# Making the low halves of the output projection's weights on VectorE, not with adding DMAs

## The chip, the cores and the metric

The kernel runs on one core of one Trainium2 chip. A core has TensorE (PE: matmuls, with a separate weight load, PEld), VectorE (DVE), ScalarE (ACT), GpSimd (POOL) and SyncE (SP); they run side by side, each through its own list of instructions in order, and wait for each other by semaphores. DMAs are issued from the queues of SP, ACT and POOL; those that add to what stands at their target are issued by POOL. Matmuls read SBUF and write PSUM, which has eight banks here of 128 x 512 numbers. The metric is device microseconds of one execution, and less is better.

## The reference

All arrays are 32-bit floats. x has 2048 tokens of 512 numbers. Two branches are computed from it and mixed token by token with a gate:

```python
g = sigmoid((x * gate_w).sum(-1, keepdims=True))
a = A(x, wqkv, wo)      # attention: 32 heads of 16; each token sees itself and the 7 tokens
                        # 2, 4, ..., 14 places back; softmax; then (heads side by side) @ wo
b = (gelu(x @ w_gate) * (x @ w_up)) @ w_down      # inner width 1792
out = g * a + (1 - g) * b
```

wo, with which this change deals, is 512 x 512: the output projection of the attention.

## The kernel before, in words

**Two-part products.** [...] Each product is three matmuls: high x high, high x low, low x high. So every weight and every intermediate result that goes into a matmul is first split, by one of two ways:
- `split` (lines 86 to 94): ScalarE copies the number into the high tile (L90, or L135 where the copy is made by `held`), then VectorE subtracts high from number into the low tile (L91).
- `split_by_dma` (lines 232 to 236): ScalarE writes the negated number's high part into the low tile (L234), a DMA issued by POOL adds the number to it (L235), and ScalarE copies the high part (`held`, L135). VectorE has no part in it.

**Stages.** Tokens are worked on in two halves (`par` 0 and 1). For each: keys and queries, values, and the feed-forward (`ffn`, 14 blocks of its inner width), in which the gate and up products (`product`, L781, in a scheme of Strassen's kind with seven products per block) and the down products (`down`, L830) alternate. Four PSUM banks named p serve these products in turn and four named acc collect. A p bank is free again when ScalarE has copied it out: by L786, L792, L882 or L898 after the gate and up products, by L845 after a group of down products. L824 is the other way: ScalarE fills a p bank from SBUF so that a further group of down products can add to it.

**Attention** is VectorE's: `scores`, `exps`, `shares` and `mix` handle a unit of 128 columns (8 heads) at a time, four units per half. `attention` is a generator, pulled piece by piece (`pull`) by the feed-forward, and fills VectorE beside the matmuls. `mix` multiplies the shares with v (L585), sums (L589, L591, L593), and after each half unit transposes (L598) and writes the result to DRAM (SP's queue, L600, four DMAs). v has one buffer, which SP loads for the next unit (L523, L524) once the reading of the last one is over.

**Output projection.** `fetch_o` brings wo into one of the two buffers named raw. `load_o`, a generator that is pulled during the last feed-forward block, splits its four parts of 128 rows (units u = 0 to 3), two into a g1 buffer and two into S buffers. `channels` loads a unit's attention result from DRAM (L1040, SP's queue, into the next raw buffers) and splits it (L90, L91). `out_first` projects the first half of the tokens, `finish` the second half: there the matmuls of `by_unit` (L1062) add to the banks that hold the feed-forward's result, and the very last ones are those of unit 3.

The buffers named raw are two. The one with wo in it becomes free when the last split of wo has read it, and takes the results of the attention after that.

**What sets the order.** The kernel is written with a scheduling layer: the order in which instructions stand in the code gives priorities, a model of times inside that layer orders each engine's list, and it adds the waits. `paced` ties an instruction to the last matmul written so far, `keep_in_program_order` and `behind` pin single ones. So one instruction more or less moves others on all engines from that place on. Everything before the split of wo stands in the same order in both versions.

Of the kernel before, what the change touches and what calls it, by code (L numbers as in the profile page):

```python
# [48 lines left out]
def tile_gated_mix(ctx: ExitStack, tc: tile.TileContext, xt, wqkv, wff, wo, out):  # L49
    nc = tc.nc  # L50
# [10 lines left out]
    def tl(tag, dt=F32):  # L61
        return pool.tile([P, COLS.get(tag, 512)], dt, name=tag, bufs=BUFS[tag])

    def pair(tag):
        t = tl(tag, F32R)
        return t[:, :512], t[:, 512:1024]
# [19 lines left out]
    def split(eng, hi, lo, raw, copy=None, pinned=False):  # L86
        if copy:
            copy(hi, raw)
        else:
            nc.scalar.activation(hi, raw, AF.Copy)  # L90
        ins = eng.tensor_tensor(lo, raw, hi.bitcast(F32), op=OP.subtract)  # L91
        if pinned or PIN[0]:
            tc.keep_in_program_order(ins)
        return ins
# [39 lines left out]
    def held(o, i):  # L134
        ins = paced(nc.scalar.activation(o, i, AF.Copy))  # L135
        LAST_HI[:] = [ins]
        return ins
# [94 lines left out]
    def split_by_dma(hi, lo, raw):  # L232

        paced(nc.scalar.activation(lo, raw, AF.Copy, scale=-1.0))  # L234
        nc.gpsimd.dma_start(lo.bitcast(F32), raw, accum_op=OP.add)  # L235
        held(hi, raw)
# [371 lines left out]
    def paced(ins):  # L608

        if PIN[0] and ins.ins.engine == mybir.EngineType.DVE:  # L610
            tc.keep_in_program_order(ins)
        if not PACING[0]:
            return ins
        tc.add_manual_dep(ins.ins, LAST[-1].ins.name, mybir.DependencyInfo(mybir.DependencyClass.Sync,
                          mybir.DependencyReason.SCHED_ONLY), reason="pace")
        return ins
# [167 lines left out]
    def copy(ps):  # L784
        s = tl("s")
        nc.scalar.activation(s, ps, AF.Copy)  # L786
        return s
# [160 lines left out]
    def ffn(par):  # L948
        todo = iter(())
        for f in range(FC):  # L950
# [23 lines left out]
            if par:  # L974
                if f + 2 < FC:
                    at(0, fetch_sums, f + 2)
                else:
                    at(0, fetch_o) if f + 2 == FC else None
                if f + 1 == FC:
                    todo = chain(load_o(), channels_of(0, 0))  # L980
                    for i in range(1, 9):
                        at(i, next, todo, None)
            else:
                if f + 2 < FC:
                    at(1, fetch, f + 2)
                    at(8, combine, f + 2)
                else:
                    at(0, fetch_x, 1, f + 2 - FC)
                if f + 1 < FC:
                    do.setdefault(0, []).insert(0, lambda: keep(f + 1))  # L990
                at(0, keep_parts, f)
                if f + 2 == FC:
                    at(8, early)
                if f + 1 == FC:
                    todo = before()
                    for i in range(2, 9):
                        at(i, next, todo, None)
# [26 lines left out]
    def load_o():  # L1024
        t = tl("g1", F32R)
        cols = [t[:, i * 512:(i + 1) * 512] for i in range(4)]
        for u in range(NU):
            raw = WO[u]
            WO[u] = hi, lo = pair("S") if u > 1 else cols[2 * u:2 * u + 2]
            split_by_dma(hi, lo, raw)  # L1030
            yield

    OR = []
# [89 lines left out]
    for kc in range(KC):  # L1123
# [4 lines left out]
        raw = QR[name, i] = spare[i] if kc > 1 else tl("rt")  # L1128
# [218 lines left out]
```

## Time and profile before

| | |
|---|---|
| median of 3 runs | 596.75 us (595.22 to 597.41) |
| profiled execution | 597.42 us |
| its span, first to last instruction | 595.4 us |
| TensorE busy | 587.3 us, 99% |
| VectorE busy | 532.3 us, 89% |
| ScalarE busy | 427.5 us, 72% |
| mean granted clock of TensorE | 0.996 |
| DMA, mean | 240 GB/s |

How to read the lines that follow in the prediction: in a timeline, a line has the start and the duration in microseconds, the engine (PEq, SPq and so on are the queue's own issuing), the line of the code, the operation, the tile it writes and those it reads (without buffer numbers), and the count where several equal ones follow each other. In brackets stands the idle time of the engine just before it and what ended it. Starts of neighbours on one engine lie closer than the durations say, since an engine starts the next instruction before the last one is through. A chain of waits goes back from the last instruction to what released it, step by step. A line of the view by windows gives busy time and count per engine in that stretch, and the clock that TensorE was granted, as a share of full speed.

### The profile page before, as it was taken

What the parts mean: (1) busy time and instruction counts of PE and PEld (TensorE: products, weight loads), DVE (VectorE), ACT (ScalarE), POOL (GpSimd) and SP (SyncE); (2) the same over time, 40 slices, a digit from 0 to 9 for tenths busy, and PEclk for the clock granted to TensorE, in tenths of its full rate; (3) what the DMA queues carried; (4) which work ended last, traced back from release to release, by engine and by line L of the source; (5) the groups of instructions that cost most, each with busy time, mean ns of one, the idle gap of its engine ahead of it and who ended that gap; (6) DMA issues with size and microseconds to landing.
All of it is one profiled execution on the core that took longest, in us unless ns stands there. A gap on an engine that the chain in (4) does not pass through costs nothing.

```text
span 595.4 us, 8273 instructions
## 1 busy us (share of the span) xinstructions
PE 587.3 (99%) x2743; PEld 489.9 (82%) x2743; DVE 532.3 (89%) x623; ACT 427.5 (72%) x756; POOL 130.2 (22%) x157
## 2 busy tenths in 40 slices
PE   8999999999999999999999999999999999989997
PEld 6889888888888888888799888888888888868885
DVE  6889998999899995998997999998999899897871
ACT  6777667778887779877777665778767867795432
POOL 0140751112111212113120860112111113131300
PEclk9999999999999999999999999999999999998999
DMA  8689999988987979899999999869798988568934
GB/s 306 217 248 280 299 310 226 304 197 233 282 218 232 266 213 255 245 253 347 273 267 355 225 270 272 260 167 275 176 273 242 217 251 214 159 132 213 187 71 159
DMA packets 88424, 142.76 MB, mean 240 GB/s; under 512 B 8639, under 2 KB 49983, under 8 KB 88382
## 3 DMA queue, kind: packets, MB, share of 16 engines
q1 hardware_dynamic: 65454, 103.21, 52.3%
q0 software_dynamic: 22640, 38.64, 35.3%
q8 instruction: 21, 0.34, 0.2%
q10 hardware_dynamic: 288, 0.39, 0.2%
q14 instruction: 21, 0.17, 0.1%
HBM read 69.83 MB, written 46.49 MB: 195 GB/s over the span
## 4 chain that ended last, share of the span: by engine, by line
PE 95%; ACT 3%; DMA 1%; SPq 0%; issue 0%; ACTq 0%
PE p L781 43%; PE p L830 13%; PE acc L830 12%; PE acc L478 10%; PE p L1062 6%; PE p L364 4%; PE acc L364 3%; PE p L478 2%; PE acc L1062 2%; DMA raw<-xt 1%; ACT A L90 1%; ACT L898 0%; SPq L1132 0%; ACT g L234 0%; ACT hh L807 0%
## 5 line engine op out<-in xcount | busy, mean ns | idle before, releaser
L781 PE MATMUL p<-S,g 128*128 128x512 f32 x672 | 167.0, 389 | 0.0
L781 PEld LDWEIGHTS p<-S,g 128*128 128x128 f32 x672 | 125.8, 188 | 25.8
L781 PE MATMUL p<-A,g 128*128 128x512 f32 x504 | 125.8, 389 | 0.0
L781 PEld LDWEIGHTS p<-A,g 128*128 128x128 f32 x504 | 94.4, 188 | 19.8 <-ACT rt L845 0.3
L585 DVE TENSOR_TENSOR prod<-v,lg 128x2048 f32<-128x2048 f32 x32 | 72.7, 2273 | 2.3 <-DMA v<-vs 2.1
L542 DVE TENSOR_REDUCE lg<-prod 128x128 f32<-128x2048 f32 x32 | 73.0, 2281 | 0.2
L539 DVE TENSOR_TENSOR prod<-kq 128x2048 f32<-128x2048 f32 x32 | 72.9, 2277 | 0.2
L830 PE MATMUL p<-d,hh 128*128 128x512 f32 x224 | 68.5, 389 | 0.0
L830 PE MATMUL acc<-d,hh 128*128 128x512 f32 x224 | 59.2, 389 | 0.0
L740 POOL DMA_DIRECT2D g<-raw x26 | 23.6, 907 | 160.2 <-ACT g L737 103.6
L792 ACT ACTIVATE c<-p 128x512 f32<-128x512 f32 x56 | 33.4, 597 | 34.0 <-PE p L781 33.9
L830 PEld LDWEIGHTS acc<-d,hh 128*128 128x128 f32 x224 | 42.0, 188 | 8.7
L830 PEld LDWEIGHTS p<-d,hh 128*128 128x128 f32 x224 | 42.0, 188 | 8.8
L830 PE MATMUL p<-d,hl 128*128 128x512 f32 x112 | 42.1, 389 | 0.0
L793 DVE TENSOR_TENSOR c<-c,s 128x512 f32<-128x512 f32 x56 | 37.8, 681 | 4.6 <-ACT c L792 4.2
L797 DVE TENSOR_TENSOR c<-c 128x512 f32<-128x512 f32 x56 | 38.1, 683 | 2.1 <-ACT c L898 2.0
L589 DVE TENSOR_TENSOR prod<-prod 128x1024 f32<-128x1024 f32 x32 | 38.9, 1217 | 0.1
L845 ACT ACTIVATE rt<-p 128x512 f32<-128x512 f32 x48 | 27.7, 595 | 15.0 <-PE p L830 14.8
L786 ACT ACTIVATE s<-p 128x512 f32<-128x512 f32 x56 | 33.2, 595 | 5.5 <-PE p L781 5.1
L478 PE MATMUL acc<-d,S 128*128 128x512 f32 x144 | 35.6, 390 | 0.1
L772 POOL DMA_DIRECT2D d<-r x23 | 19.8, 859 | 68.9 <-ACT d L771 41.7
L830 PE MATMUL acc<-d,hl 128*128 128x512 f32 x112 | 34.6, 389 | 0.0
(223 smaller groups left out, 1068.3 us busy)
## 6 DMA issues: line engine op xcount, KB each, us to landing
g<-raw POOLq DMA_DIRECT2D x26, 512.0 KB, 6.7
ws<-g SPq DMA_DIRECT2D x14, 768.0 KB, 6.2
g<-ws SPq DMA_DIRECT2D x14, 768.0 KB, 6.6
r<-wff SPq DMA_DIRECT2D x28, 256.0 KB, 4.2
raw<-wff SPq DMA_DIRECT2D x14, 512.0 KB, 4.6
d<-r POOLq DMA_DIRECT2D x23, 256.0 KB, 6.6
ws<-raw SPq DMA_DIRECT2D x14, 384.0 KB, 5.7
raw<-ws SPq DMA_DIRECT2D x14, 384.0 KB, 3.8
```

The source lines that it names most:

```text
L364: LAST[:] = [nc.tensor.matmul(ps[:, :n], x[:, ts], VO[b][w][:, kc * WQ:kc * WQ + n], start=first, stop=(kc == 1 and i == 2), skip_group_ch ...
L478: LAST[:] = [nc.tensor.matmul(ps, x[:, ts], w, start=(start and kc == i == 0), stop=(kc == 1 and i == 2), skip_group_check=True)]
L539: paced(nc.vector.tensor_tensor(prod, spans(k, jj), q[:, jj:jj + 2, None, :].to_broadcast([P, 2, W, UC]), op=OP.mult))
L542: nc.vector.tensor_reduce(two_of(lg, jj), prod.rearrange("p j w (h d) -> p (j w) h d", d=DH), axis=AX.X, op=OP.add)
L585: paced(nc.vector.tensor_tensor(prod.rearrange("p j w (h d) -> p (j w) h d", d=DH), spans(v, jj).rearrange("p j w (h d) -> p j w h d", d=D ...
L589: nc.vector.tensor_tensor(prod[:, :, :4], prod[:, :, :4], prod[:, :, 4:], op=OP.add)
L781: LAST[:] = [nc.tensor.matmul(ps, w_, a_, start=(start and kc == 0 and n == 0), stop=(kc == 1 and n == 2), skip_group_check=True)]
L792: nc.scalar.activation(c, ps, AF.Copy)
L793: nc.vector.tensor_tensor(c, c, s, op=OP.add)
L797: nc.vector.tensor_tensor(ge, ge, up, op=OP.mult)
L830: LAST[:] = [nc.tensor.matmul(pp, a[:, ts], w, start=(i == 0 and n == 0 and gr == 0), stop=(i == 1 and n == 2), skip_group_check=True)]
L1062: LAST[:] = [nc.tensor.matmul(pa, a, b, start=(first and n == 0), stop=(last and n == 2), skip_group_check=True)]
```

## The change

`load_o` calls `split` with VectorE's subtraction in place of `split_by_dma`, with the same copy (`held`) for the high part. For each of the four parts of wo the negating copy L234 on ScalarE and the adding DMA L235 on POOL's queue are gone, and one subtraction L91 on VectorE is there.

```diff
         for u in range(NU):
             raw = WO[u]
             WO[u] = hi, lo = pair("S") if u > 1 else cols[2 * u:2 * u + 2]
-            split_by_dma(hi, lo, raw)
+            split(nc.vector, hi, lo, raw, held)
             yield
```

```python
    def split(eng, hi, lo, raw, copy=None, pinned=False):
        if copy:
            copy(hi, raw)
        else:
            nc.scalar.activation(hi, raw, AF.Copy)
        ins = eng.tensor_tensor(lo, raw, hi.bitcast(F32), op=OP.subtract)
...
    def split_by_dma(hi, lo, raw):

        paced(nc.scalar.activation(lo, raw, AF.Copy, scale=-1.0))
        nc.gpsimd.dma_start(lo.bitcast(F32), raw, accum_op=OP.add)
        held(hi, raw)
```

The lists of instructions are the same up to the first of these, and differ from there to the end. Three places:

TensorE, where the last gate and up products end and the output projection begins (both versions in one, - for before and + for now; g_5106 is the last block's weight, g_5191 the first two parts of wo, A the attention's result, d and hh, hl the operands of the down products):

```order
 L781 MATMUL p<-S,g_5106 128x512 x6
+L830 MATMUL p<-d,hh 128x512 x2
+L830 MATMUL p<-d,hl 128x512
+L830 MATMUL p<-d,hh 128x512 x2
+L830 MATMUL p<-d,hl 128x512
 L1062 MATMUL p<-g_5191,A 128x512 x6
 L1062 MATMUL p<-S,A 128x512 x5
```

A group of six down products, which stood behind the first two groups of the projection, now comes ahead of them.

ScalarE at the same place, before (S_5253 is the last part of wo, p_5205 and p_5179 are banks with products of the last block, p_5293 and p_5328 banks of down products):

```order
L135 ACTIVATE S_5239<-raw_5048 128x512
L234 ACTIVATE S_5253<-raw_5048 128x512
L135 ACTIVATE S_5253<-raw_5048 128x512
L90 ACTIVATE A_5323<-raw_5266 128x4x4x32
L805 ACTIVATE hl_5227<-c_5223 128x512
L807 ACTIVATE hh_5226<-c_5223 128x512
L882 ACTIVATE c_5263<-p_5186 128x512
L90 ACTIVATE A_5341<-raw_5266 128x4x4x32
L792 ACTIVATE c_5283<-p_5205 128x512
L845 ACTIVATE rt_3956<-p_5293 128x512
L824 ACTIVATE p_5328<-rt_3981 128x512
L792 ACTIVATE c_5315<-p_5179 128x512
```

And now (the same instructions have other numbers: p_5204 was p_5205, p_5324 was p_5328, S_5250 was S_5253):

```order
L135 ACTIVATE S_5237<-raw_5048 128x512
L135 ACTIVATE S_5250<-raw_5048 128x512
L90 ACTIVATE A_5319<-raw_5262 128x4x4x32
L882 ACTIVATE c_5259<-p_5186 128x512
L90 ACTIVATE A_5337<-raw_5262 128x4x4x32
L805 ACTIVATE hl_5225<-c_5221 128x512
L807 ACTIVATE hh_5224<-c_5221 128x512
L824 ACTIVATE p_5324<-rt_3981 128x512
L792 ACTIVATE c_5279<-p_5204 128x512
L845 ACTIVATE rt_3956<-p_5289 128x512
L792 ACTIVATE c_5311<-p_5179 128x512
L90 ACTIVATE S_5435<-raw_5436 128x4x4x32
```

The L234 is gone, L882 stands ahead of L805, and L824, which fills the bank for that group of down products, stands ahead of the two L792 and not between them.

VectorE at the end of the last attention unit, before (prod_5420 is the unit's fourth and last round; hl_5673 is the low part of the unit's first block of results, hl_5678 that of its last, and hl_5639 and hl_5644 are of the unit ahead of it):

```order
L593 TENSOR_TENSOR o_5398<-prod_5399 128x4x64
L585 TENSOR_TENSOR prod_5420<-v_5302,lg_4792 128x2048
L589 TENSOR_TENSOR prod_5420<-prod_5420 128x2x512
L91 TENSOR_TENSOR hl_5639<-raw_5636,hh_5638 128x4x4x32
L91 TENSOR_TENSOR hl_5644<-raw_5636,hh_5643 128x4x4x32
L591 TENSOR_TENSOR prod_5420<-prod_5420 128x2x256
L91 TENSOR_TENSOR hl_5673<-raw_5636,hh_5672 128x4x4x32
L593 TENSOR_TENSOR o_5398<-prod_5420 128x4x64
L598 STREAM_TRANSPOSE tb_5305<-o_5398 128x512
L91 TENSOR_TENSOR hl_5678<-raw_5636,hh_5677 128x4x4x32
```

And now (the fourth round is prod_5416; hl_5640 was hl_5644, hl_5669 was hl_5673, hl_5674 was hl_5678):

```order
L589 TENSOR_TENSOR prod_5395<-prod_5395 128x2x512
L91 TENSOR_TENSOR hl_5640<-raw_5632,hh_5639 128x4x4x32
L591 TENSOR_TENSOR prod_5395<-prod_5395 128x2x256
L593 TENSOR_TENSOR o_5394<-prod_5395 128x4x64
L91 TENSOR_TENSOR hl_5669<-raw_5632,hh_5668 128x4x4x32
L585 TENSOR_TENSOR prod_5416<-v_5298,lg_4792 128x2048
L589 TENSOR_TENSOR prod_5416<-prod_5416 128x2x512
L591 TENSOR_TENSOR prod_5416<-prod_5416 128x2x256
L593 TENSOR_TENSOR o_5394<-prod_5416 128x4x64
L598 STREAM_TRANSPOSE tb_5301<-o_5394 128x512
L91 TENSOR_TENSOR hl_5674<-raw_5632,hh_5673 128x4x4x32
```

The subtractions of the unit ahead stand a round earlier, and the one of the unit's own first block stands ahead of its last round and not near that round's end.

Further up on VectorE, the four new subtractions stand one by one among the second round of the unit before, ahead of that round's transposition. The one of the attention result for the first half of the tokens that stood there, and the additions L797 and L801 of the feed-forward, keep their places among each other. On SP's queue the loads L1040 that fill the freed raw buffer stand ahead of the four writes L600 of that transposition, and no longer behind them.

## The prediction

> **What bounds the kernel now.** I read the page first, for the engine that carries the span, then who made it wait, and then the timelines of all engines around the few waits that were left.
>
> The page: span, busy time of TensorE, its granted clock in 40 slices, and the chain that ended last.
>
> ```profile
> span 595.4 us, 8273 instructions
> PE 587.3 (99%) x2743; PEld 489.9 (82%) x2743; DVE 532.3 (89%) x623; ACT 427.5 (72%) x756; POOL 130.2 (22%) x157
> PEclk9999999999999999999999999999999999998999
> PE 95%; ACT 3%; DMA 1%; SPq 0%; issue 0%; ACTq 0%
> ```
>
> TensorE is the bound: busy for 99%, and 95% of the chain. The change removes no matmul, so it can gain only where TensorE waits or runs below its clock; both happen in one place, the slice with an 8. The first of these lines is the longest wait in the view of TensorE's waits, and the next two are TensorE on both sides of it in the timeline (start, duration, operation).
>
> ```profile
> PE p L1062 <- ACT c L792: 2.4, 1, 2.4
> 531.28 1.52 PE L781 MATMUL p<-S,g 128*128 128x512 f32 x6
> 535.19 2.04 PE L1062 MATMUL p<-g,A 128*128 128x512 f32 x6 [2.39 <-ACT c L792]
> ```
>
> At 532.80 TensorE ends the feed-forward's product, and the first matmul of the output projection finds no free PSUM bank until ScalarE has copied one out (L792). The clock, by windows of the same trace:
>
> ```profile
> core 0: us, PE busy (x) PEld busy (x) DVE busy (x) ACT busy (x) POOL busy (x), PEclk, DMA share, GB/s
> 532.86:536.28 3.42, 1.09 (x5) 0.91 (x6) 3.21 (x5) 3.42 (x8) 0.86 (x1) 1.00 1.10 204
> 536.28:539.69 3.41, 3.41 (x10) 2.63 (x9) 0.99 (x2) 0.35 (x1) 0.00 (x0) 0.50 0.65 139
> 535.15:592.00 56.85, 56.30 (x240) 46.10 (x240) 39.02 (x47) 25.80 (x44) 6.91 (x8) 0.97 0.65 155
> 547.07 16.32 PE p L1062 x72
> 588.61 0.61 PE L1062 MATMUL p<-S,hh 128*128 128x512 f32 x2
> 591.11 0.39 PE L1062 MATMUL p<-S,hl 128*128 128x512 f32 x1
> ```
>
> A stretch of 3.42 us in which TensorE worked for 1.09 is followed by one of 3.41 at clock 0.50, which loses 3.41 x 0.50 = 1.71 us. The chain's row of 72 matmuls gives a pitch of 16.32/72 = 0.2267 us; 240 matmuls remain, and 239 x 0.2267 = 54.18 against 591.11 - 535.19 = 55.92 leaves 1.74. So nothing else is lost up to the end: the place costs 2.39 us of idleness and 1.71 us of clock.
>
> [...]
>
> **ScalarE's part.** Before, ScalarE runs without a pause from 524.44 to the copy that frees the bank:
>
> ```profile
> 524.44 0.62 ACT L234 ACTIVATE g<-raw 128x512 fp32r<-128x512 f32 x1
> 524.96 0.62 ACT L135 ACTIVATE g<-raw 128x512 fp32r<-128x512 f32 x1
> 528.89 0.60 ACT L824 ACTIVATE p<-rt 128x512 f32<-128x512 f32 x1
> 534.53 0.60 ACT L792 ACTIVATE c<-p 128x512 f32<-128x512 f32 x1
> ```
>
> The change removes four L234 instructions, 0.52 us of ScalarE each (524.96 - 524.44), all between these rows. In the new order an L824 for the second feed-forward group stands at the place of that L792, and its matmuls are what TensorE does next. It starts at 534.53 - 4 x 0.52 = 532.45, ends at 533.05, and with the 0.06 us that TensorE took before (535.13 to 535.19) TensorE resumes at 533.11: **2.08 us earlier**. The pause is then 0.3 us. The L792 follows 0.52 us behind and is done at 533.57, while TensorE has six matmuls (1.36 us) to do, so no second pause opens. A pause of 0.3 us leaves TensorE busy for nine tenths of any such stretch, so I take the half clock to go: **1.71 us**. TensorE alone would then end 3.79 us earlier, its last matmul starting at 587.32.
>
> **The four adding DMAs.** Their 1 MB of moving and POOL's four issues go. They also held the weights' buffer: the next loads into it, on SP's queue, waited for the last of them. The rows are POOL's last such issue, SP's load, and VectorE's waits in this stretch.
>
> ```profile
> 531.86 0.86 POOL L235 DMA_DIRECT2D S<-raw x1 [0.19 <-issue]
> 537.29 7.51 SPq L1040 DMA_DIRECT2D raw<-os x9
> 527.51 0.69 DVE L797 TENSOR_TENSOR c<-c 128x512 f32<-128x512 f32 x1 [0.78 <-ACT c L898]
> 534.68 0.69 DVE L91 TENSOR_TENSOR A<-raw,A 128x512 fp32r<-128x512 f32 x1 [0.21 <-ACT A L90]
> 540.84 0.69 DVE L91 TENSOR_TENSOR S<-raw,S 128x512 fp32r<-128x512 f32 x1 [3.48 <-ACT S L90]
> 544.97 2.28 DVE L585 TENSOR_TENSOR prod<-v,lg 128x2048 f32<-128x2048 f32 x1
> 550.12 1.89 DVE L91 TENSOR_TENSOR hl<-raw,hh 128x512 fp32r<-128x512 f32 x3
> 551.92 0.41 DVE L593 TENSOR_TENSOR o<-prod 128x256 f32<-128x256 f32 x1
> ```
>
> **VectorE's part, first half.** It gets four subtractions. Three such take 551.92 - 550.12 = 1.80, so 0.60 each and 2.40 in all. In the new order they are done by about 531, and the buffer is free then: SP's loads go some 6 us earlier than 537.29, and the wait of 3.48 goes. Up to the attention's L585 at 544.97, VectorE had idled for 0.78 + 0.21 + 3.48 = 4.47. It now does 2.40 more, and an L797 and an L801 that stood behind that L585 come ahead of it (1.20). It also waits once more: by the pitches of the rows it reaches the addition on L792's tile at 532.6, which is there at 533.57 (1.0). In all 2.40 + 1.20 + 1.0 - 4.47 = +0.1: L585 starts at about 545.1. It ends the reading of v for attention unit 2, so the load of v for unit 3 starts as before. All the subtractions that the projection's matmuls need are done by 532.6, before TensorE asks at 534.5; the added work costs nothing here, and its cover is the idleness that goes.
>
> **VectorE's part, second half.** Here I expect some of the gain to be given back. The last attention unit on VectorE and its way through DRAM before, with SP's queue at both of its blocks:
>
> ```profile
> 547.64 0.45 SPq L524 DMA_DIRECT2D v<-vs x1
> 555.19 2.29 DVE L585 TENSOR_TENSOR prod<-v,lg 128x2048 f32<-128x2048 f32 x1 [2.11 <-DMA v<-vs]
> 559.96 2.29 DVE L585 TENSOR_TENSOR prod<-v,lg 128x2048 f32<-128x2048 f32 x1
> 564.73 0.71 DVE L598 STREAM_TRANSPOSE tb<-o 128x512 f32<-128x512 f32 x1
> 565.47 1.87 SPq L600 DMA_DIRECT2D os<-tb x4
> 569.61 0.34 SPq L1040 DMA_DIRECT2D raw<-os x1
> 570.57 2.29 DVE L585 TENSOR_TENSOR prod<-v,lg 128x2048 f32<-128x2048 f32 x1
> 576.90 0.71 DVE L598 STREAM_TRANSPOSE tb<-o 128x512 f32<-128x512 f32 x1
> 577.64 1.75 SPq L600 DMA_DIRECT2D os<-tb x4
> 580.85 0.34 SPq L1040 DMA_DIRECT2D raw<-os x1
> 584.17 0.69 DVE L91 TENSOR_TENSOR hl<-raw,hh 128x512 fp32r<-128x512 f32 x1 [6.56 <-ACT hh L90]
> ```
>
> The last transposition led to the last subtraction in 584.17 - 576.90 = 7.27 us, and its result, at 584.86, was there 4.2 us before TensorE came to it (the third of the twelve matmuls from 588.61, at 589.06). With TensorE 3.79 us earlier only 0.4 is left of that.
>
> And the new order makes VectorE later. One subtraction comes ahead of the first transposition: 0.60, of which 0.12 fills a pause between dependent steps, so 565.2. The stretch to the next L585 took 570.57 - 564.73 = 5.84 and gets one more subtraction net, so 571.55. There the new order has the subtraction of the unit's own first block, ahead of the unit's last L585 and no longer behind it. Its data must go through DRAM: at the last block's 7.27 it can start at 572.5; with SP's 4.14 from write to read (565.47 to 569.61) in place of 3.21 (577.64 to 580.85), at 573.4. VectorE waits there for 0.9 to 1.9. Then 0.60 for it, 4.77 from L585 to transposition (one round, 559.96 - 555.19), 7.27 to the last subtraction, 0.69 for it and 0.06: TensorE gets the last low part at 585.9 to 586.8. It wants it at 587.32 - 9 x 0.2267 = 585.28, and waits 0.6 to 1.5.
>
> **The sum.** 3.79 less 0.6 to 1.5 is 2.3 to 3.2 us, of which I take the middle, 2.7, since other DMAs are less dense there than before but not gone. The profiled execution took 597.42 (span 595.4 and 2.0 around it), which gives 594.2 to 595.1, and 594.7. Against the median shown, 596.75, the profiled one was slow, and the shortest, 595.22, lies 2.2 below it; some of these may not have met the half clock, which no row shows. I put the median after at **594.8**.
>
> **Rivals.**
> 1. *TensorE keeps the whole gain.* For it: a load of v that lands about 1.5 us sooner, or quicker ways through DRAM, would hide the new wait. Against it: the subtraction stands in VectorE's order ahead of the last L585, whatever the DMAs do. 597.42 - 3.79 = 593.6.
> 2. *The other side: the load of v lands late and VectorE's end becomes the bound.* The landing times of this line's loads over the trace:
>
> ```profile
> DMA to landing us min/median/max: 4.6/6.8/10.8
> ```
>
> Here VectorE had it 555.19 - 547.64 = 7.5 us after the issue. Each microsecond more goes straight to the end. From 7.5 + 2.7 = 10.2 the gain is gone; at 10.8 the time is 594.7 + 3.3 = 598.0, slower than before. For it: the output's adding DMAs now start earlier and more evenly beside that load; against it: the median is 6.8, below what it took here.
> 3. *The half clock comes back at the end.* TensorE's new wait of up to 1.5 us could do what 2.33 of 3.42 us idle did. A half-clock stretch loses 1.71 at most, and 12 x 0.2267/2 = 1.4 if it covers no more than the time of the twelve matmuls: 594.7 + 1.4 = 596.1. Against it: TensorE would be busy for more than half of the stretch that holds the wait.
> 4. *The change doesn't do what it says:* the pause at 532.8 stays, because ScalarE, which waits for VectorE's additions on the way (its L805 needs one), comes to that L824 no sooner. Then the late end of VectorE lies in TensorE's slack of 4.2 us, and the time is about 597. Against it: that addition, at 527.51 before, was itself waiting for ScalarE.
> 5. *The half clock has another cause than the pause and stays.* Then 2.08 is won, TensorE wants the last low part 1.71 later, at 586.99, and doesn't wait: 595.3. [...] Against it: the pause is TensorE's only one between the start and the end, and the half clock follows it at once.
>
> **How the numbers follow.** Forecast 0.53, rival 1 0.17, rival 2 0.11, rival 3 0.10, rival 4 0.05, rival 5 0.04. The range must take in rival 1 (593.6, with a little below for DMAs) and rivals 3 and 4 up to 597, and leaves out most of rival 2: 593.3 to 597.3. The forecast's own range is 594.2 to 595.4. Half a per cent, about what a measurement of this kernel can tell from no change, is 3.0 us: faster than 593.8 takes most of rival 1 and, if the runs beside it fall like the profiled one, a third of the forecast: 0.34. Slower than 599.7 needs more than rival 2's price, so of it only the worst, and what I don't see: 0.09. The rest, 0.57, lies within.
>
> **What would show it.** In the changed kernel's profile: TensorE's wait at about 532.8 is under 0.6 us, and the slice with an 8 is a 9; a subtraction L91 on VectorE waits 1 to 2 us for ScalarE's hh at about 572; TensorE waits 0.6 to 1.5 us at about 585 for ScalarE's hh or VectorE's hl; SP's load raw<-os moves from 537.3 to about 531. The prediction is wrong if the clock halves in any slice after the start, if v lands after 557, or if a wait of TensorE over 0.6 us stands anywhere else.

## The result and the profile after

The changed kernel takes **593.64 us** (median of 6 runs, 593.12 to 594.03); the kernel before took 597.0 beside it (6 runs, 595.22 to 597.41). The ratio is 0.995 with a 95% interval of 0.9935 to 0.9964: about 3.4 us by the medians, and by the interval 0.36 to 0.65%, on both sides of the half per cent that the prediction took as what a measurement can tell. The profiled execution took 593.55, against 597.42 before. The time lies inside the range of 593.3 to 597.3, but outside the forecast's own 594.2 to 595.4; it stands where rival 1 put it, at 593.6.

The page of the changed kernel answers the first fence of the prediction: span, busy time, TensorE's clock in 40 slices, and the chain that ended last.

```profile
span 591.8 us, 8265 instructions
PE 585.9 (99%) x2743; PEld 489.4 (83%) x2743; DVE 534.5 (90%) x627; ACT 425.4 (72%) x752; POOL 126.7 (21%) x153
PEclk9999999999999999999999999999999999999999
PE 95%; ACT 2%; DMA 1%; SPq 1%; issue 0%; ACTq 0%
```

The slice with an 8 is gone. TensorE's waits are these, the longest three of the view:

```profile
PE p L76 <- DVE warm L73: 1.0, 1, 1.0
PE p L478 <- ACT p L1155: 0.6, 1, 0.6
PE p L830 <- ACT p L824: 0.3, 1, 0.3
```

The first two stand at the start of the program, at 1.00 and 11.42 us. The wait of 2.4 us for L792 has become one of 0.3 for L824, and there is none at the end. The clock, by the two windows that were shown of before:

```profile
532.86:536.28 3.42, 3.12 (x14) 2.57 (x15) 2.62 (x3) 3.26 (x7) 0.38 (x1) 1.00 0.95 272
536.28:539.69 3.41, 3.41 (x17) 2.83 (x16) 3.41 (x6) 2.17 (x4) 0.00 (x0) 1.00 1.07 323
```

TensorE is busy for 3.12 of the first 3.42 us (1.09 before), and the second stretch runs at 1.00 in place of 0.50, with 17 matmuls in place of 10. The timeline, engine after engine, with TensorE and ScalarE at that place, then SP's and GpSimd's queues, then VectorE's last attention unit and the end:

```profile
531.31 1.52 PE L781 MATMUL p<-S,g 128*128 128x512 f32 x6
533.16 0.73 PE L830 MATMUL p<-d,hh 128*128 128x512 f32 x2 [0.33 <-ACT p L824]
...
532.50 0.61 ACT L824 ACTIVATE p<-rt 128x512 f32<-128x512 f32 x1
533.02 0.61 ACT L792 ACTIVATE c<-p 128x512 f32<-128x512 f32 x1
...
531.17 2.71 SPq L1040 DMA_DIRECT2D raw<-os  x6
547.36 0.43 SPq L524 DMA_DIRECT2D v<-vs  x1
563.98 1.76 SPq L600 DMA_DIRECT2D os<-tb  x4
567.13 0.34 SPq L1040 DMA_DIRECT2D raw<-os  x1
...
546.19 0.86 POOL L1080 DMA_DIRECT2D out<-s  x1 [2.67 <-ACT s L1079]
548.10 0.86 POOL L1080 DMA_DIRECT2D out<-r  x1 [1.05 <-ACT r L1079]
...
533.66 0.69 DVE L793 TENSOR_TENSOR c<-c,s 128x512 f32<-128x512 f32 x1 [0.98 <-ACT c L792]
544.68 2.29 DVE L585 TENSOR_TENSOR prod<-v,lg 128x2048 f32<-128x2048 f32 x1
553.22 2.29 DVE L585 TENSOR_TENSOR prod<-v,lg 128x2048 f32<-128x2048 f32 x1 [1.38 <-DMA v<-vs]
563.24 0.71 DVE L598 STREAM_TRANSPOSE tb<-o 128x512 f32<-128x512 f32 x1
570.45 0.69 DVE L91 TENSOR_TENSOR hl<-raw,hh 128x512 fp32r<-128x512 f32 x1 [0.92 <-ACT hh L90]
575.82 0.71 DVE L598 STREAM_TRANSPOSE tb<-o 128x512 f32<-128x512 f32 x1
583.18 0.69 DVE L91 TENSOR_TENSOR hl<-raw,hh 128x512 fp32r<-128x512 f32 x1 [6.65 <-ACT hh L90]
...
585.45 0.39 PE L1062 MATMUL p<-S,hl 128*128 128x512 f32 x1
587.49 0.39 PE L1062 MATMUL p<-S,hl 128*128 128x512 f32 x1
```

TensorE resumes at 533.16, 2.03 us earlier than before, and its last matmul starts at 587.49, 3.62 earlier (591.11 before). VectorE's last low part is ready at 583.18 + 0.69 = 583.87; the matmul that reads it first is that of 585.45. So 1.58 us are left there, where the prediction had TensorE wait for 0.6 to 1.5.

### The profile page after: what moved, and what is told of

It is laid out like the page before. It is cut to its first block, busy times and chain, and to the rows that moved or that the text cites. A ratio compares the mean times of both kernels' runs of the same rounds, so it can differ in the third digit from the quotient of the medians.

```text
span 591.8 us, 8265 instructions
## 1 busy us (share of the span) xinstructions
PE 585.9 (99%) x2743; PEld 489.4 (83%) x2743; DVE 534.5 (90%) x627; ACT 425.4 (72%) x752; POOL 126.7 (21%) x153
## 4 chain that ended last, share of the span: by engine, by line
PE 95%; ACT 2%; DMA 1%; SPq 1%; issue 0%; ACTq 0%
PE p L781 44%; PE p L830 13%; PE acc L830 12%; PE acc L478 10%; PE p L1062 6%; PE p L364 4%; PE acc L364 3%; PE p L478 2%; PE acc L1062 2%; DMA raw<-xt 1%; ACT A L90 0%; SPq L1132 0%; SPq L1129 0%; ACT L898 0%; ACT hl L805 0%
## 5 line engine op out<-in xcount | busy, mean ns | idle before, releaser
L585 DVE TENSOR_TENSOR prod<-v,lg 128x2048 f32<-128x2048 f32 x32 | 72.8, 2274 | 1.6 <-DMA v<-vs 1.4
L792 ACT ACTIVATE c<-p 128x512 f32<-128x512 f32 x56 | 33.4, 597 | 33.5 <-PE p L781 33.4
L797 DVE TENSOR_TENSOR c<-c 128x512 f32<-128x512 f32 x56 | 38.2, 684 | 1.2 <-ACT c L898 1.2
```

The source lines that it names most:

```text
L585: paced(nc.vector.tensor_tensor(prod.rearrange("p j w (h d) -> p (j w) h d", d=DH), spans(v, jj).rearrange("p j w (h d) -> p j w h d", d=D ...
L792: nc.scalar.activation(c, ps, AF.Copy)
L797: nc.vector.tensor_tensor(ge, ge, up, op=OP.mult)
```

## The experiments

Two theories of where the gain comes from. Theory S: from ScalarE, whose four instructions of 0.52 us were late work ahead of the copy that frees a bank, and from the half clock behind the pause of 2.39 us. Theory D: from the adding DMAs, which held a buffer and took DMA time. Besides these, three readings of the profile are tested: that VectorE's chain at the end has 1.6 us to spare, why v came sooner, and whether the pause makes the half clock.

One thing is needed to read the times below. In some executions the DMA that makes a low part hl in the middle of the program lands late; in the profiles of the runs e2, e4a, e9a and e10b TensorE waits 3.05, 3.15, 1.1 and 1.4 us for it, so their later rows stand 1 to 5 us further back, and their medians are what counts.

### ScalarE's instructions or the DMAs

**e1**: the negated copies are put back on ScalarE, nothing else.

```diff
-            split(nc.vector, hi, lo, raw, held)
+            paced(nc.scalar.activation(lo, raw, AF.Copy, scale=-1.0)); split(nc.vector, hi, lo, raw, held)
```

> The changed kernel (VectorE subtracts, no adding DMAs) with the four negated copies of ScalarE put back ahead of the subtractions; each writes the low part's tile, which the subtraction then overwrites, so nothing of the computation changes. Theory S (the gain is ScalarE's four 0.52 us instructions: they release the PSUM bank late, and the pause brings the half clock): TensorE pauses again for ScalarE's L792 by 2.0 to 2.5 us at about 533, the granted clock falls to about 0.5 for some 3.4 us behind it, and the time is 596.5 to 597.3, as before. Theory D (the gain is the adding DMAs' going: earlier free buffers, a quicker load of v): the time stays at 593.3 to 594.2. In between, about 595.3: the pause is back without the half clock.

Measured: 596.74 us (11 runs), ratio to before 0.998 (0.9951 to 1.001). Its timeline, and the clock in two windows:

```profile
534.92 1.76 PE L1062 MATMUL p<-g,A 128*128 128x512 f32 x6 [2.41 <-ACT c L792]
...
534.26 0.60 ACT L792 ACTIVATE c<-p 128x512 f32<-128x512 f32 x1
```

```profile
532.51:534.92 2.41, 0.00 (x1) 0.01 (x1) 2.41 (x4) 2.41 (x6) 0.77 (x1) 1.00 0.48 137
534.92:540.52 5.60, 5.60 (x17) 4.43 (x18) 5.60 (x8) 3.10 (x6) 0.08 (x1) 0.70 1.04 299
```

The DMAs are gone here, VectorE subtracts, and SP's first load into the weights' buffer goes out early, at 532.57. The pause is back at 2.41, and so is the half clock, and most of the gain is lost. It came in 5 of the 11 runs (mean clock 0.996, 596.8 to 597.9); the other six, at 0.998 or more, have a median of 595.3, the value named for a pause without it. Beside runs of the kernel before with the same clock (597.4 and 596.1) that is still 0.5 and 0.8 us less.

**e2**: the kernel before, with the negated copies on VectorE; the adding DMAs stay. Its order on ScalarE at the place is that of the changed kernel.

```diff
-            split_by_dma(hi, lo, raw)
+            paced(nc.vector.tensor_scalar(lo, raw, -1.0, None, op0=OP.mult)); nc.gpsimd.dma_start(lo.bitcast(F32), raw, accum_op=OP.add); held(hi, raw)
```

> The kernel before with its adding DMAs, but the four negated copies made by VectorE in place of ScalarE; nothing of the computation changes. Theory S: ScalarE is relieved just as in the changed kernel, TensorE's pause at about 533 is under 0.6 us, the granted clock stays at 1.0, and the time is 593.3 to 594.2, or up to 594.9 if the load of v is as late as before (its wait ending at about 555.2, not 553.2) and the last low part then comes 0.6 to 1.3 us too late for TensorE. Theory D: the gain goes with the DMAs, and the time is 596.5 to 597.3.

Measured: 593.76 us (13 runs), ratio 0.9939 (0.9911 to 0.9968), with a mean clock of 0.998 or more in all runs. TensorE resumes after 0.32 us:

```profile
538.15 0.73 PE L830 MATMUL p<-d,hh 128*128 128x512 f32 x2 [0.32 <-ACT p L824]
```

All but 0.1 us of the gain is there with all of the DMAs, and in e1 little of it without them. Theory D falls as the main cause. A small part is left to it: the time outside the span, from the first instruction to the last, has medians of 1.92 to 2.04 us in the versions with adding DMAs L235 (the kernel before, e2, e4a, e5, e10a) and of 1.75 to 1.84 in those without. The rest of the 0.5 and 0.8 us in e1 isn't explained.

**e5**: half of the change, VectorE for units 0 and 1 only.

```diff
-            split_by_dma(hi, lo, raw)
+            split(nc.vector, hi, lo, raw, held) if u < 2 else split_by_dma(hi, lo, raw)
```

> Half of the change: VectorE subtracts for the first two of the four units' weights, while the other two keep ScalarE's negated copies (the two L234 at 529.89 and 530.93 in the profile before) and the adding DMAs; nothing of the computation changes. Theory S: L792 starts two instructions earlier than before, at about 533.5, and TensorE pauses 1.2 to 1.5 us; such a pause leaves the clock at 1.0, so the time is that of the changed kernel plus the 1.0 us more of pause, 594.4 to 595.0. If a pause of that length brings the half clock too, 1.7 us more, 596.0 to 596.7. If the gain goes with the adding DMAs, two of four of them give half of it, 595.0 to 595.5, with the pause as short as in the changed kernel or the clock at half.

Measured: 594.94 us (8 runs, 594.52 to 595.22), ratio 0.9958 (0.9945 to 0.9971), a mean clock of 0.999 or 1.0 in all.

```profile
533.56 1.66 PE L1062 MATMUL p<-g,A 128*128 128x512 f32 x6 [1.36 <-ACT c L792]
```

The pause is 1.36, between 0.33 and 2.39 as two of four instructions say, and there is no half clock. 593.64 + 1.36 - 0.33 = 594.67 accounts for the time within 0.3.

### The slack of VectorE's last chain

**e8a** makes the last transposition three times, **e8b** five times (in the diff's place 5); both are the changed kernel otherwise.

```diff
-                nc.vector.transpose(t, o.rearrange("p b t c -> p (b t c)"))
+                for _ in range(3 if (par, u, jj) == (1, NU - 1, NP - 2) else 1): nc.vector.transpose(t, o.rearrange("p b t c -> p (b t c)"))
```

> The changed kernel with VectorE's last transposition (L598, the last unit) made three times in place of once, into the same tile; nothing of the computation changes. The two added take about 0.64 us each on the chain that ends in VectorE's last low part. If that chain has the 1.6 us of slack that the profile shows (low part ready at 583.87, wanted at 585.45), the low part is ready at about 585.2, TensorE waits for nothing and the time is that of the changed kernel, 593.3 to 594.0. If the chain decides the end already, the time is 1.2 to 1.4 us longer, 594.7 to 595.2.

Measured: 594.08 us (12 runs), 0.4 above the changed kernel and 0.1 above the range expected, with a span of 591.8 in the profile, the same as that of the changed kernel.

```profile
575.69 2.20 DVE L598 STREAM_TRANSPOSE tb<-o 128x512 f32<-128x512 f32 x3
584.64 0.69 DVE L91 TENSOR_TENSOR hl<-raw,hh 128x512 fp32r<-128x512 f32 x1 [1.59 <-ACT hh L90]
585.39 0.50 PE L1062 MATMUL p<-S,hl 128*128 128x512 f32 x1
```

The low part comes at 585.33, and the matmul that reads it starts at 585.39: the slack is used up to the last tenth, and in this profile costs nothing until then.

> The changed kernel with VectorE's last transposition (L598, the last unit) made five times in place of once; nothing of the computation changes. Four more at about 0.75 us each (2.20 us for three, by the run with three) put the last low part 3.0 us later, at about 586.9, which is 1.4 us behind the 585.45 at which TensorE wants it. If the slack of 1.6 us is what kept the gain whole, TensorE waits 1.2 to 1.6 us at about 585.5 and the time is 594.7 to 595.4. If that chain has no say in the end, the time stays at 593.3 to 594.1.

Measured: 595.93 us (10 runs, from 595.13), ratio to before 0.9996 (0.9971 to 1.0021). TensorE's timeline at the place:

```profile
585.40 0.39 PE L1062 MATMUL acc<-S,hl 128*128 128x512 f32 x1
587.27 0.73 PE L1062 MATMUL p<-S,hh 128*128 128x512 f32 x2 [1.48 <-ACT hh L90]
590.17 0.39 PE L1062 MATMUL p<-S,hl 128*128 128x512 f32 x1
```

TensorE's wait of 1.48 has the size expected, and in this execution the clock stays at 1.00 through it. (Two of the ten runs, at 596.86 and 602.46, have a mean clock of 0.997, and the profiled executions with a half-clock stretch behind the pause have 0.996 or 0.997; no profile caught one of the two.) The time is 0.5 above what was expected: the last twelve matmuls take 590.17 - 587.27 = 2.90 from the first start to the last, against 587.49 - 585.00 = 2.49 in the changed kernel, since behind the high part TensorE waits 0.4 more, in small pieces, for the low part. That makes 593.64 + 1.48 + 0.41 = 595.53; the last 0.4, as in e8a, isn't explained. So this chain is the next bound, and the changed kernel is 1.6 us away from it.

### Why v came sooner

The output's adding DMAs (L1080, 256 KB each, GpSimd's queue) go out at other times in the changed kernel, since TensorE and ScalarE come to the projection's tiles earlier. In the kernel before, two stood close ahead of the load of v at 547.64:

```profile
546.31 0.86 POOL L1080 DMA_DIRECT2D out<-s  x1 [12.03 <-ACT s L1079]
546.88 1.18 POOL L1080 DMA_DIRECT2D out<-r  x1
551.47 0.86 POOL L1080 DMA_DIRECT2D out<-s  x1 [3.41 <-ACT s L1079]
```

In the changed kernel one stands ahead of it, 1.17 us, and the next 0.74 behind. **e10a** is the kernel before without the first two.

```diff
-                nc.gpsimd.dma_start(out_v[2 * jj], r, accum_op=OP.add)
+                if jj > 1: nc.gpsimd.dma_start(out_v[2 * jj], r, accum_op=OP.add)
```

> The kernel before without the first two of GpSimd's eight adding DMAs from L1080 (two tiles of the first block's projection are not added to the output, which is left incomplete by them); they go out 1.33 and 0.76 us ahead of the load of v in the profile before. If it is these two, going out together, that make the load of v take 7.5 to 8.2 us from its issue to VectorE's start, as in the kernel before, and not 5.7 to 5.9, as in the changed kernel, it takes 6.3 us or less. If the load is slowed by something else (SP's loads ahead of it, its own place), it stays at 7.3 to 8.3. The time is 597 in either case, or about 595.5 where the half clock does not come, since TensorE waits for nothing of it.

Measured: 597.46 us (8 runs), ratio 1.0017 (0.9996 to 1.0038). The view of DMA issues between 545 and 558 gives, by issue, size and the time from issue to landing; first the kernel before, then the changed one, then this run:

```profile
v<-vs SPq DMA_DIRECT2D x1, 512.0 KB, 7.5
```

```profile
v<-vs SPq DMA_DIRECT2D x1, 512.0 KB, 5.8
```

```profile
v<-vs SPq DMA_DIRECT2D x1, 512.0 KB, 4.7
```

And VectorE in this run, now without any wait for v:

```profile
553.24 2.25 DVE L585 TENSOR_TENSOR prod<-v,lg 128x2048 f32<-128x2048 f32 x1
```

Two adds 0.8 and 1.3 us ahead of it: 7.5 us (7.8 to 8.1 in three more profiles of the same kernel). None: 4.7. With the order of all engines the same as before, SP's loads among them, the two adds are the cause of the slow load. For other spacings there are only the profiles of the other runs. The load took 5.5 to 5.9 us in the five where one add goes out 0.8 to 1.2 us ahead and the one before it at least 3.5 us ahead (the changed kernel, e7c, e8a, e8b, e10b). It took 6.5 in e2 (adds 3.0 and 5.1 us ahead), 6.9 in e1 (2.4 and 3.5) and 7.9 in e5 (2.4 and 3.0). So the number of adds in the last microsecond doesn't decide it: two close together and 2.4 us or more ahead were as bad as two just ahead. The time doesn't move, because before the change TensorE had 4.2 us to spare at the end.

**e10b** was to be the converse: the changed kernel with one more add close ahead of the load.

```diff
-                nc.gpsimd.dma_start(out_v[2 * jj], r, accum_op=OP.add)
+                for _ in range(2 if jj == 2 else 1): nc.gpsimd.dma_start(out_v[2 * jj], r, accum_op=OP.add)
```

> The changed kernel with the third of GpSimd's adding DMAs from L1080, the one that goes out 1.17 us ahead of the load of v, issued twice in a row (that tile is added to the output twice, which changes it). If two adds going out together are what makes the load of v slow, it takes 7.2 to 8.2 us in place of 5.7 to 5.9, VectorE starts on v at 554.6 to 555.6, some 2 us later, its last low part comes up to 0.4 us too late, and the time is 593.5 to 594.4. If adds have no say in it, the load stays under 6.3 us and the time at 593.3 to 594.1.

Measured: 593.14 us (4 runs), ratio 0.9948 (0.9929 to 0.9967). It missed its target: the second add of tile 2 changes the same rows as the first, at 547.64, and so waits until that one has landed (the 1.98 us in brackets); it went out well behind the load, together with the next tile's add:

```profile
548.80 0.42 SPq L524 DMA_DIRECT2D v<-vs  x1
...
552.38 1.75 POOL L1080 DMA_DIRECT2D out<-s  x2 [1.98 <-DMA out<-s]
...
554.37 2.29 DVE L585 TENSOR_TENSOR prod<-v,lg 128x2048 f32<-128x2048 f32 x1 [1.09 <-DMA v<-vs]
```

It tells nothing of an add ahead of the load; 3.6 us behind its issue one more add left VectorE's start at 5.6 us from it.

### The pause and the half clock

**e4a**: the kernel before with the last product ahead of the pause issued twice, so that matmuls fill a part of it.

```diff
-        product(X_, "s3", w["t3"], False)
+        for _ in range(2 if par and f == FC - 1 else 1): product(X_, "s3", w["t3"], False)
```

> The kernel before, with the six matmuls of TensorE's last product ahead of its pause (the product s3 of the second block's last chunk) issued twice; the product is then accumulated twice, which changes the output, and it adds 1.36 us of matmuls where TensorE waits 2.39 us for a PSUM bank. Theory S (the pause brings the half clock): the pause shrinks to about 1.0 us, TensorE takes up again at the same time (about 535.2), the granted clock stays at 1.0, and the time is 595.0 to 595.6, that is 1.4 to 2.0 us under the kernel before, though six matmuls more run. Rival (the half clock has another cause, such as the long stretch of full load or the matmul form behind it): the stretch at 0.5 stays, and the time is 596.7 to 597.3; rival (a pause of 1.0 us is enough for it too): the same.

Measured: 596.6 us (12 runs), ratio 1.0 (0.9962 to 1.0038). The place in its profile, and the clock behind it:

```profile
537.94 2.88 PE L781 MATMUL p<-S,g 128*128 128x512 f32 x12
541.85 1.66 PE L1062 MATMUL p<-g,A 128*128 128x512 f32 x6 [1.03 <-ACT c L792]
```

```profile
541.85:548.00 6.15, 6.15 (x27) 5.08 (x28) 3.87 (x8) 2.90 (x6) 0.00 (x0) 1.00 0.89 224
```

The pause is 1.03 and the clock full, as theory S has it, and of the 12 runs nine have a mean clock of 0.999 or more (the other three stand at 601.0 to 603.7; the profile caught one of them, and there the half clock came behind the late DMA's wait of 3.15 us). But the nine have a median of 596.36 and not 595.0 to 595.6. The kernel before at full clock has 596.1 to 596.4 (below), so the two agree, and it was the gain from a full clock that was set too high, by about 0.8 us. Why is not known: no profile shows the kernel before at full clock.

**e7c**: the changed kernel with three of the four copies back, for a pause between 1.36 and 2.4.

```diff
-            split(nc.vector, hi, lo, raw, held)
+            [paced(nc.scalar.activation(lo, raw, AF.Copy, scale=-1.0)) for _ in (0,) if u > 0]; split(nc.vector, hi, lo, raw, held)
```

> The changed kernel with three of ScalarE's four negated copies put back ahead of the subtractions (those of the last three units; each writes what the subtraction overwrites, so nothing of the computation changes). TensorE pauses for L792 by 1.7 to 2.0 us, between the 1.36 us at which the clock stayed at 1.0 in all runs with two left and the 2.4 us at which it fell in part of them. If a pause of this length never brings the half clock, the time is 593.6 + 1.6 = 595.0 to 595.6 in all runs, with a mean clock of 0.998 or more. If it does as the 2.4 us do, part of the runs stand at 596.7 to 597.4 with a mean clock of 0.996 to 0.997.

Measured: 595.46 us (10 runs, 594.56 to 603.45), ratio 0.9984 (0.995 to 1.0018).

```profile
534.51 1.66 PE L1062 MATMUL p<-g,A 128*128 128x512 f32 x6 [1.88 <-ACT c L792]
```

The pause is 1.88. Six runs stand at 594.56 to 595.66 with a mean clock of 0.998 or more, the profiled one among them, three at 596.33 to 597.62 with 0.996 or 0.997, and one at 603.45 with 0.993. So, by the mean clocks, this pause of 1.88 us brought the half clock in a part of its executions. With four, three, two and none of the instructions the pauses are 2.39, 1.88, 1.36 and 0.33: 0.51 to 0.52 us for each. The first three have the projection ahead on TensorE, as before, and the last the down products, so TensorE's new order has no share of its own in the pause.

**e9a, e9b, e9c**: the kernel before, three more profiles.

> The kernel before, unchanged, profiled once more: its runs fall into two groups, about 596.1 with a mean granted clock of 0.998 to 1.0 and about 597.2 with 0.996 to 0.997. If the half clock comes only in part of the executions behind the same pause, a profile of the first group shows the pause of 2.3 to 2.5 us at about 533 as before, but a clock of 1.0 behind it. If the first group differs by its pause, the pause is under 1.5 us there. A profile of the second group shows what was seen before: 2.4 us, then 3.4 us at 0.5.

> The same as the run ahead of it, for a second chance at the other group: pause of 2.3 to 2.5 us in both groups if the clock answers to it by chance, and a pause under 1.5 us in the group at full clock if it answers to the pause's length alone.

> The kernel before, unchanged, profiled once more, for an execution of its other group (about 595.3 to 596.2, mean granted clock 0.998 or more): a pause of 2.3 to 2.5 us at about 533 as before and a clock of 1.0 behind it if the clock falls by chance behind the same pause; a pause under 1.5 us there if the pause's length decides. Otherwise the 2.4 us and some 3.4 us at 0.5 once more.

Measured: 599.16, 597.4 and 597.19 us. All three show the half clock, so the other group was not caught. But they show that it starts at different times. TensorE's timeline in the last one, and the clock by windows:

```profile
535.12 2.93 PE L1062 MATMUL p<-g,A 128*128 128x512 f32 x6 [2.39 <-ACT c L792]
```

```profile
531.38:534.79 3.41, 1.35 (x6) 0.77 (x5) 3.20 (x4) 3.41 (x8) 1.94 (x3) 1.00 0.97 187
534.79:538.21 3.42, 3.09 (x7) 2.48 (x8) 2.41 (x4) 1.77 (x4) 0.00 (x0) 0.50 0.82 140
```

Here the clock falls at 534.79, while TensorE still waits (the pause runs from 532.73 to 535.12), and comes back at 538.21. In the profile before it fell 1.09 us after the pause's end.

## Why the prediction was right, and where it was not

**What bounds it, and ScalarE's part: right.** The pause and the half clock were the only losses. L824 was to start at 532.45 and did at 532.50; TensorE was to resume at 533.11 and did at 533.16; a pause of 0.3 was foretold and is 0.33. The half clock went. TensorE's last matmul was to start at 587.32 without a wait at the end, and starts at 587.49. e1, e2 and e5 show that ScalarE's four instructions are the cause; e2 has all but 0.1 us of the gain.

**The four adding DMAs: right in their place, and worth next to nothing.** SP's loads went out at 531.17 (about 531 foretold), VectorE's wait of 3.48 went, and e2 shows that the time is the same to 0.1 us with the DMAs still there.

**VectorE's first half: right.** A wait of 1.0 for L792's tile was foretold and is 0.98; L585 was to start at about 545.1 and does at 544.68. The four subtractions cost nothing, as said.

**VectorE's second half: the order right, one size wrong.** The subtraction of the unit's first block does stand ahead of the last L585 and VectorE does wait there, 0.92 us (0.9 to 1.9 foretold); the way from the first transposition to it took 570.45 - 563.24 = 7.21, the 7.27 of the lower end. The term that failed is the load of v: "the load of v for unit 3 starts as before" held (547.36 against 547.64), but the sum also had it land as before, with L585 at 555.19. It started at 553.22, 1.97 us sooner. That is nearly the whole distance from 585.9, the earliest that the last low part was forecast for, to the 583.87 at which it was ready. So TensorE's wait of 0.6 to 1.5 did not come, and the 2.7 us of the sum became 3.6 by the spans. The price of the load came from a single row, of a place where two adding DMAs go out just ahead of it (e10a), and the change moves just these. The prediction did name their moving, but as something that could make the load late (rival 2). It made it quicker. That the spread of the adds did this in the changed kernel is argued from e10a, which shows it for the kernel before; e10b, meant as the converse, doesn't test it. The upper end of that wait rested on a single row too, SP's 4.14 from write to read: it was 3.53 in another profile of the kernel before and 3.15 after.

**The rivals.** Rival 1 happened, by the first mechanism it named, a load of v about 1.5 us sooner, and the range held because it took in this rival. That its 593.6 was met within 0.1 us is in part luck: TensorE gained 3.62 and not 3.79, and the time outside the span, set at 2.0, was 1.8. Rival 2 did not: v landed sooner, and e8b prices the end behind it, at 2.3 us by the medians for 3.0 more on that chain. Rival 3: there was no wait at the end; in the profile of e8b, where there was one of 1.48, the clock stayed full. But two of e8b's ten runs have a mean clock of 0.997, and none of the 35 runs in which the pause is 0.33 and the end has no such wait (the changed kernel, e2, e8a, e10b), so for a wait of that size rival 3 is not ruled out. Rival 4 did not happen. Rival 5 is out for the changed kernel, where the clock is full behind a pause of 0.33, and against it speak e5 (no run of 8 with a low clock behind 1.36 us) and e4a.

**The base.** That some executions of the kernel before miss the half clock was supposed and is so. Of 71 runs of it beside the experiments, 40 have a mean clock of 0.997 or less and 31 one of 0.998 or more; the medians of the two groups in the three sets are 597.4 and 596.1, 597.6 and 596.3, 597.35 and 596.4. That is 1.0 to 1.4 between them, where a profile with the half clock shows 1.5 to 1.7 lost. Why it isn't all of it stays open.

## What to carry to other kernels

Where one engine is busy for 99%, look for its few waits and then at the engine they name: four short instructions of an engine that is busy for 72% were worth 3.4 us, because they stood ahead of a copy that frees a bank, and a megabyte of DMAs taken away was worth some 0.1 us beside them (e2). A forecast of what is given back later needs the price of a transfer in its new surroundings: list what else goes out within some microseconds of it before and after, and take the row of another place with the same company. And a loss that an execution meets or misses by chance belongs into the base as a share, not as a fixed sum.

## What was not expected of the hardware

**The half clock came in pieces of 3.41 us, and not with every pause.** In six profiles with a pause of 2.39 to 2.41 us (the kernel before, e1, e9a, e9b, e9c, e10a) it lasted 3.41 or 3.42 each time, and began between 2.1 and 3.8 us after the pause's start, from 0.33 ahead of the pause's end (e9a, e9c) to 1.39 behind it (e1); in the 3.41 ahead of its beginning TensorE had been busy for 1.02 to 1.39, that is 30 to 41%. Behind the late DMA, a pause of 3.15 (e4a) brought 6.83 at half, twice 3.41, and one of 3.05 (e2) brought none. These are two stretches of e2 with that pause, 412.55 to 415.60, in them:

```profile
410.59:414.00 3.41, 1.95 (x9) 1.30 (x7) 3.41 (x5) 3.36 (x6) 1.41 (x2) 1.00 1.03 304
414.00:417.42 3.42, 1.82 (x8) 1.53 (x9) 2.95 (x4) 2.49 (x4) 0.00 (x0) 1.00 1.07 240
```

By pause, the runs with a mean clock of 0.997 or less are: none of 35 at 0.33, none of 8 at 1.36, 2 of 10 in e8b with its 1.48 at the end, 4 of 10 at 1.88, 50 of 90 at 2.4; of these, one of the two, one of the four and seven of the 50 took over 600 us, and may owe their clock to the late DMA.

How a pause can miss it is an estimate and not shown. In the profile of the kernel before, the clock stays at 1.00 from the end of the half clock at 539.69 to a second fall at 594.31, behind the last matmul: 54.6 us, or 16 times 3.41. If the clock can change only every 3.41 us, and the pause does not move these borders, then a border can cut a pause in two. The two stretches of e2 above meet inside the pause: TensorE is busy for 57% of the first and 53% of the second, more than the 30 to 41% ahead of the six falls, and the clock is 1.00 in both and up to 420. That a border lies at 414.00 there is not shown, since no change of the clock marks it. A pause of 2.4 us cut near its middle would leave some 65% on each side (3.41 less 1.2) and could be missed too; nor is it shown that the executions of the kernel before at full clock are of this kind, since none was profiled. For the way back there are two measurements: in e4a the first 3.42 us at half clock had TensorE busy for 2.44, 71%, and the next 3.41 stayed at half, while in e9c 3.09 of 3.42, 90%, were followed by the full clock.

**Two DMAs that add slowed a load beside them by 2.8 us**: taking away two adds of 256 KB close ahead of a load of 512 KB brought it from 7.5 us to 4.7 (e10a). With the adds spread out it took 5.5 to 5.9, and with two close together up to 3.0 us ahead still 7.9 (e5).
